# Delta-rule attention and GELU MLP on one NeuronCore: two units per join product, and the small products gathered into fewer stretches of TensorE work

## The chip, the cores and the metric

The kernel runs on one core of a Trainium2 chip. The metric is the device time of one execution in microseconds (us); the kernel before took 667.81 us, the median of 3 executions between 667.59 and 668.14. All the profile's times are of one profiled execution whose span was 667.6 us.

## The reference

Two blocks follow each other, all in float32. The first is a delta-rule recurrence for 4 batches x 8 heads, 768 steps, head size 48. The second is an MLP over the 3072 tokens, 384 -> 2048 -> 384, with an exact GELU.

```python
k_n = k / (norm(k) + 1e-06)
state = zeros(B, H, D, D)
for t in range(S):
    y[:, :, t] = q_t @ state
    v_old = state @ k_t
    state = state + beta_t * outer(k_t, v_t - v_old)
x = y.transpose(0, 2, 1, 3).reshape(B * S, H * D)
out = gelu(x @ w_in) @ w_out
```

## The kernel before, in words

**Chunks.** The 768 steps are cut into 12 chunks of C = 64. Within a chunk the recurrence is solved in closed form: the Gram matrix K K^T (`grams`), a unit triangular system built from it, the products of keys and queries with the running state (`against_state`), the solve itself (`solve`), the masked Q K^T (`queries`) times the solution, and the state's update (both in `outputs`, through `use`). A "unit" is one batch and head in one chunk. 32 units (2 chunks, 4 batches, 8 heads) make a group, and two batches lie above each other in the 128 partitions: partitions 0 to 63 hold one, 64 to 127 the other. In the code a tile index `u.a` is a pair of batches, `u.t` the place in the group, and `p` picks the half of the partitions.

**The triangular inverse.** For each group VectorE inverts all 32x32 diagonal blocks at once, one elimination row after another (`eliminate_steps`, L442 and L444). The missing off-diagonal 32x32 block of each unit is then made from two small products, the "joins". Level 0 multiplies the Gram block by the inverse of the upper diagonal block, and VectorE scales it into `xm` (L528). Level 1 multiplies that by the inverse of the lower block, and ScalarE copies it into the solve's matrix `zf` (L532). `join_steps` makes three calls of `join_run`: level 0 of the group's first chunk (call it J0), level 0 of its second chunk with level 1 of the first (J1), and level 1 of the second chunk (J2). Each product is a 32x32 by 32x32 matmul (L520).

**The MLP.** `fc1` (L684) makes 32 blocks of the hidden layer for a chunk's 256 tokens, each of three accumulating 128x128 by 128x256 matmuls. From chunk 2 on the second layer runs as seven block products (Strassen's scheme) of 16 matmuls of 128x128 by 128x192 each (L722). Its sums are on VectorE.

**Order.** `ffn_steps`, `state_steps`, `eliminate_steps` and the rest return lists of steps. `at(first, last, steps)` gives each a due time in chunks (w + 0.23 is about a quarter into the time of chunk w), and `emit` traces them all sorted by due time. VectorE then keeps exactly that order (`manual_schedule` for DVE). For TensorE and ScalarE the trace order is a priority: a list scheduler picks the first instruction that it holds ready. So a small product whose operand or PSUM buffer isn't free at that moment lets MLP matmuls in ahead of it, and a sequence of small products can come apart.

**PSUM.** All small products write into tiles tagged `dn` of two banks each, and there are two such tiles. A third one in flight waits until one has been read out. `queries`, `grams`, `solve` and each set of `join_run` take one; `against_state` and `use` take one per pair of batches, so two.

**In time of an even chunk w** the order is: J0 and the Gram product of chunk w+2 at w+0.23, J1 at w+0.30, J2 and Q K^T of chunk w at w+0.36, and then `state_steps`: keys and queries against the state (below: A), the solve (S), the outputs (O) and the transposition for the MLP. **In time of an odd chunk** it is the Gram product of chunk w+2 and Q K^T of chunk w at w+0.09, then A, S, O. Between these stand the MLP's matmuls. The keys reach the matmuls through a transposition on VectorE (`turned_k`, L352) into `Kt`, of which there are six buffers, two per chunk.

Of the kernel before, what the change touches and what calls it, by code (L numbers as in the profile page):

```python
# [11 lines left out]
ALU = mybir.AluOpType  # L12
# [4 lines left out]
def kernel(  # L17
# [28 lines left out]
    nc = tc.nc  # L46
    B, H, S, D = q.shape
    DM, DF = moe_w_in.shape
    C = 64
# [19 lines left out]
    def dn(name):  # L69
        return ps.tile([128, 2, 512], F32, tag="dn", name=name)  # L70
# [433 lines left out]
    def join_run(g, ts0, ts1):  # L504

        xm, zf, off = XMs[g], Zf[g % 2], Gs[g]
        gm = gms[g].rearrange("q t h -> q (t h)")
        sets = []
        for level, ts in enumerate((ts0, ts1)):
            if ts:  # L510
                psJ = dn("psJ")[:, 0].rearrange("q (u n) -> q u n", n=HB)
                sets.append((level, slice(ts[0] * H, (ts[-1] + 1) * H), psJ))
        for i in range(2 * H):
            for p in range(2):
                for level, us, psJ in sets:
                    u = us.start + i
                    top = slice(p * C, p * C + HB)
                    low_ = slice(p * C + HB, (p + 1) * C)
                    rows, to = (top, low_) if level == 0 else (low_, top)
                    nc.tensor.matmul(psJ[to, i, :], lhsT=(xm if level else off)[rows, u, :],  # L520
                                     rhs=zf[rows, u, HB:C] if level else xm[rows, u, :],
                                     start=True, stop=True)
        for level, us, psJ in sets:
            for p in range(2):
                top = slice(p * C, p * C + HB)
                low_ = slice(p * C + HB, (p + 1) * C)
                if level == 0:
                    nc.vector.tensor_tensor(  # L528
                        xm[low_, us, :], psJ[low_],
                        gm[low_, us].unsqueeze(2).to_broadcast([HB, 2 * H, HB]), op=ALU.mult)  # L530
                else:
                    nc.scalar.copy(zf[top, us, HB:C], psJ[top])  # L532
# [12 lines left out]

    def join_steps(g):
        a, b = range(NA), range(NA, 2 * NA)
        return [(1.0, join_run, g, a, ()), (1.0, join_run, g, b, a), (1.0, join_run, g, (), b)]
# [116 lines left out]
    def state_steps(c):  # L665
        us = [tiles[c, a] for a in range(NA)]
        steps = [(3.0, against_state, us), (2.0, solve, us), (3.0, outputs, us)]
        return steps + [(0.5, turn, u) for u in us]
# [258 lines left out]
    def late():  # L927
# [3 lines left out]
        for a in range(NA):  # L931
# [3 lines left out]
            for c in range(5, NC, 2):  # L935
# [11 lines left out]
             at(2.64, 2.77, join_steps(1)), at(2.76, 2.985, state_steps(2)),  # L947
# [6 lines left out]
    for c in range(4, NC):  # L954
# [8 lines left out]
        t = {4: 2.76, 5: 2.955}.get(c, c - (1.97 if c % 2 == 0 else 2.36))  # L963
        plan += [at(t, t + 0.01, [(1.0, turned_k, u) for u in us])]
        t = c + (0.05 if c % 2 == 0 else -0.34)
        plan += [at(t, t + 0.01, [(1.0, turned_q, u) for u in us])]
    for w in range(3, NC):
        us = [tiles[w, a] for a in range(NA)]
        two_ahead = w + 2 < NC
        gram = [(1.0, grams, [tiles[w + 2, a] for a in range(NA)])] if two_ahead else []  # L970
        query = [(1.0, queries, us)]
        if w == 3:
            gram = [(1.0, transposed, u, (1,)) for u in us] + gram
        if w % 2:
            plan += [at(w + 0.09, w + 0.092, gram + query), at(w + 0.25, w + 0.95, state_steps(w))]
# [6 lines left out]
        else:  # L982
            joins = join_steps(w // 2)
            plan += [at(w + 0.23, w + 0.232, joins[:1] + gram),
                     at(w + 0.3, w + 0.302, joins[1:2]),
                     at(w + 0.36, w + 0.362, joins[2:] + query),
                     at(w + 0.39, w + 0.97, state_steps(w))]
# [35 lines left out]
```

## Time and profile before

The chunks 4 to 9 form three alike periods of two chunks (an even chunk and the odd one after it), and 10 and 11 are a shorter fourth.

| stretch of the span, us | what | length | PE busy | DVE busy | ACT busy |
|---|---|---|---|---|---|
| 75 to 145 | MLP of chunks 0 and 1, chunk 1's state | 70.0 | 69.45 | 66.18 | 34.50 |
| 145 to 225 | joins of the first planned group, chunks 2 and 3 | 80.0 | 78.22 | 63.96 | 26.39 |
| 225 to 326, one period | chunks 4 and 5 | 101.0 | 100.88 | 69.34 | 31.09 |
| 528 to 625 | chunks 10 and 11, from the joins on | 97.0 | 96.88 | 39.78 | 24.63 |

PE is the matmul row of TensorE, DVE is VectorE, ACT is ScalarE. A matmul's recorded duration runs from its start to its modelled end, and matmuls overlap, so the space between two starts tells what one costs in a stream. The small matmuls on part of the array appear twice each in the records: a set of 32 join products is a group of x64. In a line of the timeline stand the start, the length from the first start to the last end, the engine, the line of the kernel, the operation, output and inputs, array rows * columns in use, the moving operand and the count.

### The profile page before, as it was taken

What the parts mean: (1) busy time and instruction counts of PE and PEld (TensorE: products, weight loads), DVE (VectorE), ACT (ScalarE), POOL (GpSimd) and SP (SyncE); (2) the same over time, 40 slices, a digit from 0 to 9 for tenths busy, and PEclk for the clock granted to TensorE, in tenths of its full rate; (3) what the DMA queues carried; (4) which work ended last, traced back from release to release, by engine and by line L of the source; (5) the groups of instructions that cost most, each with busy time, mean ns of one, the idle gap of its engine ahead of it and who ended that gap; (6) DMA issues with size and microseconds to landing.
All of it is one profiled execution on the core that took longest, in us unless ns stands there. A gap on an engine that the chain in (4) does not pass through costs nothing.

```text
span 667.6 us, 21705 instructions
## 1 busy us (share of the span) xinstructions
PE 643.4 (96%) x9542; PEld 563.6 (84%) x9542; DVE 451.9 (68%) x921; ACT 228.5 (34%) x605; POOL 82.3 (12%) x82
## 2 busy tenths in 40 slices
PE   6877999999999999999999999999999999999997
PEld 5666776767789989989989989989989989989997
DVE  6999999994799845489846489846479844324022
ACT  3367755704432242242143142143142132122220
POOL 4050300103110021111021111021111010000000
PEclk9966999998999999999999999999999999999999
DMA  9885655303432232511332511211301210100101
GB/s 132 175 253 173 121 170 133 48 1 71 83 45 39 51 52 43 85 32 26 57 53 45 82 27 31 51 19 32 67 3 26 56 18 3 25 2 2 24 1 25
DMA packets 158431, 39.76 MB, mean 60 GB/s; under 512 B 150016, under 2 KB 153216, under 8 KB 158336
## 3 DMA queue, kind: packets, MB, share of 16 engines
q1 hardware_dynamic: 152464, 33.40, 26.5%
q10 hardware_dynamic: 5872, 4.97, 3.3%
q8 instruction: 75, 1.23, 0.8%
q14 instruction: 20, 0.16, 0.1%
HBM read 33.62 MB, written 4.72 MB: 57 GB/s over the span
## 4 chain that ended last, share of the span: by engine, by line
PE 86%; DVE 7%; ACT 3%; issue 2%; DMA 1%; SPq 0%; DVEq 0%
PE psH L684 36%; PE psX L722 12%; PE psY L722 12%; PE psO L697 5%; PE psZ L722 4%; PE psK L575 3%; PE psJ L520 3%; PE psG L367 3%; PE psU L600 2%; PE psY L618 2%; DVE Nu L444 2%; DVE tmp L442 2%; PE psY L627 1%; ACT U L606 1%; PE psX L662 1%
## 5 line engine op out<-in xcount | busy, mean ns | idle before, releaser
L684 PE MATMUL psH<-xT,w_in_sb 128*128 128x256 f32 x1152 | 261.4, 383 | 2.4 <-ACT G L686 2.3
L684 PEld LDWEIGHTS psH<-xT,w_in_sb 128*128 128x128 f32 x1152 | 215.7, 190 | 33.7 <-ACT G L686 3.5
L686 ACT ACTIVATE G<-psH 128x256 f32<-128x256 f32 x192 | 73.3, 382 | 181.8 <-PE psH L684 169.8
L444 DVE TENSOR_TENSOR Nu<-Nu,tmp 128x30 f32<-128x30 f32 (+9 forms) x180 | 62.9, 349 | 6.2
L442 DVE TENSOR_TENSOR tmp<-Nu 128x30 f32<-128x30 f32 (+9 forms) x180 | 60.5, 336 | 5.1
L722 PE MATMUL psX<-w_out_sb,G 128*128 128x192 f32 x320 | 56.2, 329 | 0.0
L722 PE MATMUL psY<-w_out_sb,G 128*128 128x192 f32 x304 | 54.1, 329 | 0.6
L722 PEld LDWEIGHTS psX<-w_out_sb,G 128*128 128x128 f32 x320 | 52.2, 190 | 0.7
L722 PEld LDWEIGHTS psY<-w_out_sb,G 128*128 128x128 f32 x304 | 49.1, 190 | 2.1 <-DVE u L768 1.8
L663 ACT COPY xT<-psX 128x384 f32<-128x384 f32 x24 | 11.4, 478 | 105.0 <-PE psX L662 105.0
L697 PE MATMUL psO<-w_out_sb,G 128*128 128x384 f32 x128 | 45.0, 498 | 0.0
L306 POOL TENSOR_TENSOR n<-n,half 128x16 f32<-128x16 f32 x10 | 29.4, 2937 | 88.2 <-DVE n L281 67.4
L402 DVE TENSOR_TENSOR P<-psG,mask 128x1024 f32<-128x1024 f32 x10 | 12.2, 1224 | 37.0 <-PE psG L367 37.0
L606 ACT COPY U<-psU 64x192 f32<-64x192 f32 x96 | 30.0, 313 | 21.0 <-PE psU L600 19.7
L697 PEld LDWEIGHTS psO<-w_out_sb,G 128*128 128x128 f32 x128 | 23.7, 191 | 14.4 <-DVE w_out_sb L236 0.6
L583 DVE TENSOR_TENSOR W<-psK,V 128x384 f32<-128x384 f32 x22 | 12.1, 552 | 28.8 <-ACT y L582 28.8
L469 POOL MEMSET Zf<- 32x512 f32 x23 | 12.4, 540 | 154.5 <-DVE Zf L457 153.6
L731 DVE TENSOR_TENSOR S<-G 128x512 f32<-128x512 f32 x20 | 13.7, 687 | 25.8 <-ACT G L686 25.7
L332 POOL TENSOR_TENSOR V<-V,n 128x384 f32<-128x384 f32 x18 | 17.3, 968 | 104.5 <-DMA V<-in_v_dram 69.2
L641 DVE TENSOR_TENSOR x<-psY,y 64x192 f32<-64x192 f32 x80 | 28.3, 354 | 0.9
L722 PE MATMUL psY<-T,G 128*128 128x192 f32 x160 | 28.2, 329 | 0.0
L722 PE MATMUL psX<-T,G 128*128 128x192 f32 x160 | 28.1, 329 | 0.0
(138 smaller groups left out, 871.4 us busy)
## 6 DMA issues: line engine op xcount, KB each, us to landing
Kp<-in_k_dram SPq DMA_DIRECT2D x76, 96.0 KB, 3.3
w_out_sb<-in_moe_w_in_dram SPq DMA_DIRECT2D x24, 256.0 KB, 4.3
V<-in_v_dram SPq DMA_DIRECT2D x48, 96.0 KB, 3.1
out_dram<-o_sb ACTq DMA_DIRECT2D x46, 96.0 KB, 2.2
w_raw<-in_moe_w_out_dram SPq DMA_DIRECT2D x10, 384.0 KB, 4.7
Zf<-in_moe_w_out_dram SPq DMA_DIRECT2D x6, 384.0 KB, 3.9
Qp<-in_q_dram SPq DMA_DIRECT2D x64, 32.0 KB, 2.1
Qp<-in_q_dram SPq DMA_DIRECT2D x16, 96.0 KB, 4.2
```

Source lines behind the costliest of these rows:

```text
L306: nc.gpsimd.tensor_tensor(flat, flat, half, op=ALU.pow)
L367: nc.tensor.matmul(psG[HALF[p], r, i * NP + j, :], lhsT=u.Kt[rows, p, j, :], rhs=(u.Qt if x else u.Kt)[rows, p, j, :], start=True, stop=True)
L442: nc.vector.tensor_tensor(tmp, nu[:, j + 1:, j:j + 1].to_broadcast([128, n, j]), nu[:, j:j + 1, 0:j].to_broadcast([128, n, j]), op=ALU.mult)
L444: nc.vector.tensor_tensor(nu[:, j + 1:, 0:j], nu[:, j + 1:, 0:j], tmp, op=ALU.add)
L520: nc.tensor.matmul(psJ[to, i, :], lhsT=(xm if level else off)[rows, u, :], rhs=zf[rows, u, HB:C] if level else xm[rows, u, :], start=True, ...
L575: nc.tensor.matmul(u.psK[to, x, r, j, :], lhsT=(u.Qt if x else u.Kt)[rows, p, j, :], rhs=St[rows, u.a, p, j, :], start=True, stop=True)
L606: copy(pairs(u.U[HALF[p]], s), u.psU[HALF[p ^ s], p])
L641: nc.vector.tensor_tensor(dst, src, pairs(u.y[HALF[p ^ s]], s), op=ALU.add)
L684: nc.tensor.matmul(psH, lhsT=w_in_sb[:, f // 2, m, f % 2 * 128:(f % 2 + 1) * 128], rhs=xTs[c][:, m, :], start=(m == 0), stop=(m == NM - 1))
L686: nc.scalar.activation(G[:, f, :], psH, ACT.Gelu)
L697: nc.tensor.matmul(u.psO, lhsT=G[:, f, u.a * 128:(u.a + 1) * 128], rhs=w_out_sb[:, f, :], start=(f == 0), stop=(f == NF - 1))
L722: nc.tensor.matmul(ps_, lhsT=lhs[:, f, :], rhs=rhs[:, f, :], start=first and f == 0, stop=f == FH - 1, skip_group_check=not first)
```

## The change

One join product takes two units. The stationary operand is two neighbouring units' blocks side by side (32 rows, 64 columns) and the moving operand two units' blocks (64 columns). Of the 64x64 result only the two 32x32 blocks on the diagonal are wanted. This halves the number of join matmuls. Both levels of J1 share one `dn` tile, a bank each, and the readouts take every other unit, twice as many instructions with half the elements each.

The helper `together` records for each TensorE instruction of its steps a dependence on the one before it, for order alone and with no semaphore, so that they are issued in this sequence. With it the small products are placed anew. Even chunk: J0 with Q K^T of w, J1 with the Gram product of w+2, J2 with A, S with the Gram product of w+3, O. Odd chunk: A, S with Q K^T of w, O. The keys of odd chunks are transposed a little earlier (c - 2.49 in place of c - 2.36). For chunk 3 the two transpositions of its queries stand ahead of the Gram product of chunk 5, and for the first planned group each join call is kept together by itself.

```diff
@@ join_run
-                psJ = dn("psJ")[:, 0].rearrange("q (u n) -> q u n", n=HB)
-                sets.append((level, slice(ts[0] * H, (ts[-1] + 1) * H), psJ))
-        for i in range(2 * H):
+        psJ = dn("psJ").rearrange("q b (k n) -> q b k n", n=2 * HB)
+        sets = [(level, ts[0] * H, psJ[:, level])
+                for level, ts in enumerate((ts0, ts1)) if ts]
+        for k in range(H):
             for p in range(2):
-                for level, us, psJ in sets:
-                    u = us.start + i
+                for level, u0, psJ in reversed(sets):
+                    us = slice(u0 + 2 * k, u0 + 2 * k + 2)
+                    rows = slice(p * C + level * HB, p * C + (level + 1) * HB)
+                    nc.tensor.matmul(psJ[HALF[p], k, :],
+                                     lhsT=(xm if level else off)[rows, us, :],
+                                     rhs=zf[rows, us, HB:C] if level else xm[rows, us, :],
...
+                for e in range(2):
+                    us = slice(u0 + e, u0 + 2 * H, 2)
+                    src = psJ[at_:at_ + HB, :, e * HB:(e + 1) * HB]
...
@@ together (new)
+        run = [next(i for i in reversed(traced) if i.engine == pe)]
...
+        for before, i in zip(run, run[1:]):
+            tc.add_manual_dep(i, before.name,
+                              mybir.DependencyInfo(mybir.DependencyClass.NoSync,
+                                                   mybir.DependencyReason.DATA),
...
@@ state_steps
-        steps = [(3.0, against_state, us), (2.0, solve, us), (3.0, outputs, us)]
+        steps = [(3.0, together, *first, (against_state, us)),
+                 (2.0, together, (solve, us), *second), (3.0, outputs, us)]
@@ the plan, odd chunks
-            plan += [at(w + 0.09, w + 0.092, gram + query), at(w + 0.25, w + 0.95, state_steps(w))]
+            plan += [at(w + 0.25, w + 0.95, state_steps(w, (), query(w)))]
@@ the plan, even chunks
-            plan += [at(w + 0.23, w + 0.232, joins[:1] + gram),
-                     at(w + 0.3, w + 0.302, joins[1:2]),
-                     at(w + 0.36, w + 0.362, joins[2:] + query),
-                     at(w + 0.39, w + 0.97, state_steps(w))]
+            plan += [at(w + 0.23, w + 0.232, [(1.0, together, j0, *query(w))]),
+                     at(w + 0.35, w + 0.351, [(1.0, together, j1, *gram(w + 2))]),
+                     at(w + 0.39, w + 0.97, state_steps(w, (j2,), gram(w + 3)))]
```

## The prediction, made before the changed kernel was run

> **What bounds the kernel now.** I read the page's busy shares first, then the table by stretches, TensorE's waits from 80 us on, and the timeline of TensorE. The page:
>
> ```profile
> PE 643.4 (96%) x9542; PEld 563.6 (84%) x9542; DVE 451.9 (68%) x921; ACT 228.5 (34%) x605; POOL 82.3 (12%) x82
> ```
>
> The stretches of the three alike periods (length, then PE, PEld, DVE, ACT, POOL busy):
>
> ```profile
> 225.00:326.00 101.00, 100.88 (x1582) 91.70 (x1581) 69.34 (x149) 31.09 (x76) 14.03 (x11) 1.00 0.30 49
> 326.00:427.00 101.00, 100.88 (x1582) 91.70 (x1581) 69.35 (x149) 31.10 (x76) 13.73 (x11) 1.00 0.30 49
> 427.00:528.00 101.00, 100.88 (x1582) 91.70 (x1581) 69.30 (x149) 30.14 (x74) 13.52 (x11) 1.00 0.19 33
> ```
>
> What TensorE waited for after 80 us:
>
> ```profile
> PE psJ L520 <- issue: 1.2, 1, 1.2
> PE psH L684 <- ACT G L686: 0.3, 1, 0.3
> ```
>
> The reader sees a period of 101.0 us with TensorE busy for all of it, at full clock, and under 2 us of matmul waits in the whole rest. Every us of TensorE's stream that goes away shortens the kernel, as long as no other engine takes over; VectorE has 32 us to spare in a period. But a busy row also holds drains and changes between array shapes. Those the timeline shows, by starts:
>
> ```profile
> 437.54 1.16 PE L367 MATMUL psG<-Kt 48*64 48x64 f32 x64
> 438.63 2.86 PE L684 MATMUL psH<-xT,w_in_sb 128*128 128x256 f32 x12
> 441.42 1.20 PE L520 MATMUL psJ<-XM,G 32*32 32x32 f32 x64
> 442.55 1.56 PE L684 MATMUL psH<-xT,w_in_sb 128*128 128x256 f32 x6
> 444.04 1.20 PE L520 MATMUL psJ<-Zf,XM 32*32 32x32 f32 x64
> ...
> 448.89 5.45 PE L684 MATMUL psH<-xT,w_in_sb 128*128 128x256 f32 x24
> 454.26 0.68 PE L575 MATMUL psK<-St,Kt 48*64 48x48 f32 x32
> 454.77 0.65 PE L575 MATMUL psK<-St,Qt 48*64 48x48 f32 x32
> 455.23 0.65 PE L575 MATMUL psK<-St,Kt 48*64 48x48 f32 x32
> 455.70 0.65 PE L575 MATMUL psK<-St,Qt 48*64 48x48 f32 x32
> ...
> 462.97 1.15 PE L600 MATMUL psU<-W,Zf 64*64 64x48 f32 x64
> 464.05 2.87 PE L722 MATMUL psX<-w_out_sb,G 128*128 128x192 f32 x16
> ```
>
> Three prices come from it. (1) *The MLP side of an interruption.* 24 first-layer matmuls take 454.26 - 448.89 = 5.37 us, 12 take 441.42 - 438.63 = 2.79, so one is 0.215 us and a stretch between two small runs has 2.79 - 12 x 0.215 = 0.20 us on top. (2) *The small side.* A block of 32 records of A takes 455.23 - 454.77 = 0.46 us, so 64 are 0.93; S, with 64, takes 464.05 - 462.97 = 1.08. Entry and exit are 0.15 us. An interruption thus costs 0.35 us beside its products. (3) *A join set.* 64 records take 442.55 - 441.42 = 1.13 us, about 1.01 of stream and 0.12 of exit.
>
> The joins have a telling exception near the end, where the two levels of J1 alternate:
>
> ```profile
> 541.33 0.21 PE L520 MATMUL psJ<-XM,G 32*32 32x32 f32 x1
> 541.34 0.21 PE L520 MATMUL psJ<-Zf,XM 32*32 32x32 f32 x1
> ...
> 542.43 0.19 PE L520 MATMUL psJ<-Zf,XM 32*32 32x32 f32 x1
> 542.55 2.86 PE L684 MATMUL psH<-xT,w_in_sb 128*128 128x256 f32 x12
> ```
>
> Here 128 records take 1.10 us to the last start, 8.6 ns each, where a lone level takes 16.0. A lone level uses two parts of the array (rows 0 and 64 upward), J1 uses four. So a part repeats every 32 to 34 ns either way: a lone join set is bound by its two parts, not by the number of instructions.
>
> **What the Trainium skill says.** "TensorE: Matmul & The Clock Gate", section "The mechanism", has weight loads overlap running matmuls only on other row groups; the 2 against 4 parts above agree. Its section "LDWEIGHTS (loading the stationary operand)" prices a load by its columns alone, columns / 1.2 ns: an estimate of 27 ns for 32 columns and 53 for 64. The trace has 32 ns per part at 32 columns; at 64 columns (A, S, O, the Gram product, four parts) 0.46 us / 32 x 4 = 58 ns with a block's seam. Both are the page's figure plus about 5, so I trust the slope. "TensorEngine Tiling (Array Packing)", "Key Properties", says that a change of tiling mode drains the array; the 0.35 us agree in kind.
>
> **The change, part by part.**
>
> *Half the join matmuls.* J0 falls from 64 records to 32 on the same two parts, but each loads 64 columns and streams 64. Not shown by the trace: 64 columns with 32 rows, where no second column part shares the rows. Bounds for a part's repeat: 32 ns if nothing grows with width, 75 if load and stream are added in full to today's 32 (32 + 27 + 16). I take 55, the value of the 64x64 products without a seam, between the page's 53 and the measured 58. Then J0 is 32 / 2 x 55 = 0.88 us, J1 64 / 4 x 55 = 0.88, J2 0.88; with exit 1.0 each. Halving the count therefore gives a lone set only 0.13 us. What gives more is that J1 stays whole: in three periods it is split today (the lines at 441.42 and 444.04), because it takes two `dn` tiles while the Gram product of w+2 holds one until J1 has let go of the old Gram matrix. Afterwards it takes one tile and the Gram product follows it. Four sets at 1.13 = 4.52 become three at 1.0: 1.5 us per period.
>
> *Fewer interruptions.* Today a period has 12: J0 with Gram, J1b, J1a, J2 with Q K^T, A, S, O; then a scrap of eight Gram records, Gram with Q K^T, A, S, O. The change asks for 8, with one more change of shape inside (J2 to A), about 0.14 us. But J2 with A wants three `dn` tiles: J2's and two of A. J2's must be read by four ScalarE copies first; today's two of 32x512 take 1.15 us, so four of half the size about 1.45. A's second half would be due 0.95 us after J2's end, so it comes some 0.6 us early. Either MLP matmuls slip in (a ninth interruption, 0.35) or TensorE waits 0.6. I take the former. Saving: 3 x 0.35 - 0.14 = 0.9 us. A period gains 1.5 + 0.9 = 2.4, less 0.1 for the seams inside S with Gram and S with Q K^T: 2.3. Three periods: 6.9.
>
> *Chunks 2 and 3.* The joins there have 256 records in 4.4 us (2.15 + 1.13 + 1.13); three sets at 1.0 save 1.4. The Gram product of chunk 5 now stands in three scraps between transpositions and Q K^T alone behind it; whole, and Q K^T behind S, saves about 3 x 0.35 = 1.0.
>
> *Chunks 10 and 11.* J1 is whole already: 1.13 + 1.22 + 1.13 become 3.0, 0.5 saved; 11 interruptions become 8 or 9, less the shape change: 0.5.
>
> Sum: 6.9 + 1.4 + 1.0 + 0.5 + 0.5 = 10.3 us, so 667.8 - 10.3 = 657.5.
>
> *Costed at nothing.* The readouts double in number. VectorE's two of 690 ns become four of about 0.42 (a 128x240 product takes 0.41): 0.3 us more, twice a period, in its 32 spare us, and J1 follows J0 by over 4 us of MLP work. ScalarE, a third busy, has 0.3 more per level 1. The earlier Gram product of w+3 needs `Kt` from VectorE at w+0.51, whose buffer A of w frees; VectorE has just waited for that A for its own W (L583), so it adds no wait. Behind S, Q K^T is read by VectorE (1.22 us) in its fixed order; elimination rows queue behind that, and the joins behind them, but today XM is ready at 433.0 and J0 starts at 436.4: 3.4 us of room. No wait is recorded by `together`, only order.
>
> **The rivals.** (a) *The narrow tile is faster than I take it* (a part repeats in 32 to 45 ns, because load and stream overlap): at 32 ns each set is 0.51, so 15 x 0.37 = 5.6 us more, 652; at 45, 655. For it: no other operation here uses these tiles. Against it: columns set the price of everything in the trace. (b) *The joins gain nothing* (75 ns, 1.2 per set, so 15 x 0.32 = 4.8 less), or as much is lost in waits of A's second half: 662. (c) *Waits take the place*: a chained run stands whole while ScalarE is behind. If J2's readout queues behind the Gram copies (442.67 to 445.01, 2.3 us) and its own 1.45, each of the four even chunks loses about 3.8 us at A. A is then not split, so the gain is 10.3 + 4 x 0.35 = 11.7 and the time 667.8 - 11.7 + 15.2 = 671, slower than before. Against it: some 5 us of MLP work lie between J1 and J2, in which ScalarE can finish the Gram copies.
>
> **How the numbers follow.** My case (with A split or briefly waiting, 656 to 659) 0.58; (a) 0.20; (b) 0.12; (c) together with smaller losses that eat most of the gain 0.10, over half of it beyond 669. The range leaves out the fastest end of (a) and the waits of (c): 652 to 663. Chances: faster 0.90, same 0.04, slower 0.06.
>
> **What would show it.** The changed timeline should have join sets of 32, 64 and 32 records at 0.9 to 1.0 us; 8 or 9 interruptions in a period of 98.7 us; J1 directly before the Gram product; MLP matmuls or 0.6 us of idle time inside A of the even chunks. A join set at 0.5 us speaks for (a). Waits of psK, psJ or psY on ScalarE, or of the joins on VectorE's rows, above 3 us a period would make the prediction wrong.

## The result, and the profile after

The changed kernel takes 670.80 us (median of 4 executions, 670.35 to 671.38); the kernel before took 667.97 us beside it (4 executions, 667.59 to 669.34). The ratio is 1.0037, with a 95% interval of 1.0023 to 1.0052. The change makes the kernel slower by 0.4%, where the prediction had 657.5 us and a range that ended at 663.

The page of the changed kernel, engines:

```profile
PE 634.2 (95%) x8902; PEld 554.6 (83%) x8902; DVE 454.1 (68%) x941; ACT 231.2 (35%) x625; POOL 82.1 (12%) x82
```

TensorE has 640 records fewer (9542 before) and is busy 9.2 us less (643.4 before), yet the span grew from 667.6 to 668.6 us. So work did go away, and waits took its place.

The counts in these views are records. Every matmul on float32 data stands there as two records, the large ones too, and a transposition as one: the code has 16 blocks of the hidden layer in a chunk, not 32, with three matmuls each, so 576 in all, and the view has 1152 records; a second-layer product has 8 matmuls and 16 records. Below, numbers of first-layer matmuls are numbers of records: six make one block, and each block is emptied by one GELU out of one of two PSUM tiles.

A stretch of one of the alike periods (length, then PE, PEld, DVE, ACT, POOL busy) shows where:

```profile
225.00:326.00 101.00, 99.21 (x1452) 90.10 (x1452) 69.02 (x153) 31.61 (x80) 13.79 (x11) 1.00 0.30 48
```

In the same 101.0 us TensorE is now busy for 99.21 and not for 100.88. What it waited for after 80 us, in the changed kernel (total, times, longest, us):

```profile
PE psH L700 <- ACT G L702: 3.1, 4, 0.9
PE psK L590 <- ACT Zf L532: 2.0, 4, 0.5
PE psJ L516 <- DVE XM L528: 1.6, 1, 1.6
```

Each of the first two lines comes four times, once for every even chunk from 4 on. L700 is the MLP's first layer, held up by the GELU (L702) that empties its PSUM tile. L590 is A, the products against the state, held up by the readout of J2 (L532). The third is J1 in the time of chunk 2.

The timeline of TensorE in the changed kernel, the even chunk whose former order the prediction showed:

```profile
437.13 1.15 PE L516 MATMUL psJ<-XM,G 32*64 32x64 f32 x32
438.21 1.16 PE L367 MATMUL psG<-Qt,Kt 48*64 48x64 f32 x64
439.30 5.45 PE L700 MATMUL psH<-xT,w_in_sb 128*128 128x256 f32 x24
444.68 0.27 PE L516 MATMUL psJ<-Zf,XM 32*64 32x64 f32 x1
...
445.76 1.16 PE L367 MATMUL psG<-Kt 48*64 48x64 f32 x64
446.86 2.86 PE L700 MATMUL psH<-xT,w_in_sb 128*128 128x256 f32 x12
450.63 3.24 PE L700 MATMUL psH<-xT,w_in_sb 128*128 128x256 f32 x12 [0.92 <-ACT G L702]
453.80 1.15 PE L516 MATMUL psJ<-Zf,XM 32*64 32x64 f32 x32
454.88 0.68 PE L590 MATMUL psK<-St,Kt 48*64 48x48 f32 x32
455.38 0.65 PE L590 MATMUL psK<-St,Qt 48*64 48x48 f32 x32
456.53 0.68 PE L590 MATMUL psK<-St,Kt 48*64 48x48 f32 x32 [0.51 <-ACT Zf L532]
```

The order is the one that was asked for: J0 with Q K^T, J1 with the Gram product, J2 with A. J0 takes 438.21 - 437.13 = 1.08 us, J1 (both levels, 64 records) 445.76 - 444.68 = 1.08, J2 1.08; each of them had been 1.13 per level. Two things are new. The 24 first-layer matmuls after the Gram product take 453.80 - 446.86 = 6.94 us, where 24 undisturbed ones, at 439.30 to 444.68, take 5.38: 1.56 us of waiting. And A's second half starts at 456.53, 1.15 us after the block before it, where blocks follow each other in 0.46 to 0.50.

One wait more shows later in the period, in the second layer of the changed kernel:

```profile
479.04 0.49 PE L677 MATMUL psX<-ident,x 128*128 128x128 f32 x3
479.65 0.92 PE L738 MATMUL psY<-w_out_sb,G 128*128 128x192 f32 x4
```

and of the kernel before, the same place:

```profile
476.76 0.49 PE L662 MATMUL psX<-ident,x 128*128 128x128 f32 x3
477.18 0.34 PE L367 MATMUL psG<-Kt 48*64 48x64 f32 x8
477.46 0.59 PE L722 MATMUL psY<-w_out_sb,G 128*128 128x192 f32 x2
```

Before, a scrap of eight Gram records stood behind the three transpositions. Now nothing does, and the next second-layer product starts late. Its operands have long been there; VectorE's read (L784) of the block of PSUM that this product overwrites ends at 479.60, just before it. That scrap, which the prediction counted as an interruption to be saved, stood where a wait shows now.

**The account of one period**, from the starts in both timelines. From J0 to J0 it was 101.01 us and is 101.33.

| term, us per period | before | after | difference |
|---|---|---|---|
| runs of small products, without A's wait | 19.09 | 17.56 | -1.53 |
| MLP side of the interruptions, 0.197 each | 12 | 8 | -0.79 |
| first layer waits behind J1 and Gram | 0 | 1.56 | +1.56 |
| A's second half waits for J2's readout | 0 | 0.69 | +0.69 |
| second layer waits where the scrap was | 0 | 0.39 | +0.39 |
| sum | | | +0.32 |

The first, third and fourth rows are read from the starts. The price of 0.197 us is the one of the kernel before, and the 0.39 us are what then remains of the large matmuls' time between O of the even chunk and A of the odd one, so these two rows are not measured apart. With that, the gain is there, 2.32 us, and 2.64 us of waits stand against it. Three periods make +0.96 of the 1.0 us by which the span grew. Chunks 2 and 3 add 0.08 (88.75 us from the first planned J0 to the next, now 88.83), and chunks 10 and 11 nothing (123.97 and 123.96 us from their J0 to the last product).

The medians differ by 2.83 us and not by 1.0, since the profiled execution of the kernel before was, by its span, the longest of its four (669.34 us), and that of the changed kernel (670.35) the shortest. Part of it shows in the record of the kernel before, with a granted clock of 0.95 from 145 to 180 us (1.00 in the changed kernel): Q K^T at 153.90 takes 1.90 us from start to start there, and 1.09 elsewhere. So the 0.08 us of chunks 2 and 3 are likely too small a loss. The lengths of the periods, which all lie at full clock, are free of this and are what the experiments are read by.

### The profile page after: what moved, and what is told of

It is laid out like the page before. It is cut to its first block, busy times and chain, and to the rows that moved or that the text cites. A ratio compares the mean times of both kernels' runs of the same rounds, so it can differ in the third digit from the quotient of the medians.

```text
span 668.6 us, 20459 instructions
## 1 busy us (share of the span) xinstructions
PE 634.2 (95%) x8902; PEld 554.6 (83%) x8902; DVE 454.1 (68%) x941; ACT 231.2 (35%) x625; POOL 82.1 (12%) x82
## 3 DMA queue, kind: packets, MB, share of 16 engines
q8 instruction: 70, 1.15, 0.7%
## 4 chain that ended last, share of the span: by engine, by line
PE 73%; DVE 15%; ACT 5%; issue 3%; DMA 2%; SPq 1%; POOL 0%; ACTq 0%; POOLq 0%; DVEq 0%
PE psH L700 31%; PE psX L738 12%; PE psY L738 12%; PE psZ L738 4%; DVE tmp L442 3%; DVE Nu L444 3%; PE psK L590 3%; PE psJ L516 2%; PE psG L367 2%; PE psU L615 2%; ACT Zf L532 2%; PE psY L633 1%; DVE w_e L235 1%; DVE w_out_sb L236 1%; PE psY L642 1%
## 5 line engine op out<-in xcount | busy, mean ns | idle before, releaser
L700 PE MATMUL psH<-xT,w_in_sb 128*128 128x256 f32 x1152 | 261.2, 383 | 5.4 <-ACT G L702 4.5
L700 PEld LDWEIGHTS psH<-xT,w_in_sb 128*128 128x128 f32 x1152 | 216.4, 191 | 39.4 <-ACT G L702 8.8
L702 ACT ACTIVATE G<-psH 128x256 f32<-128x256 f32 x192 | 73.5, 383 | 175.9 <-PE psH L700 156.4
L528 DVE TENSOR_TENSOR XM<-psJ,gm 32x256 f32<-32x256 f32 x40 | 16.8, 421 | 25.1 <-PE psJ L516 24.7
L752 DVE TENSOR_TENSOR G<-G 128x512 f32<-128x512 f32 x20 | 13.8, 692 | 24.2 <-PE psX L738 24.2
```

What stands on the lines that cost most here:

```text
L528: nc.vector.tensor_tensor(xm[low_, us, :], src, gm[low_, us].unsqueeze(2).to_broadcast([HB, H, HB]), op=ALU.mult)
L700: nc.tensor.matmul(psH, lhsT=w_in_sb[:, f // 2, m, f % 2 * 128:(f % 2 + 1) * 128], rhs=xTs[c][:, m, :], start=(m == 0), stop=(m == NM - 1))
L702: nc.scalar.activation(G[:, f, :], psH, ACT.Gelu)
```

## The experiments

Theory 1 was: the readouts of J1 on ScalarE hold up the GELUs behind them. The rivals were: the narrow tile itself is too slow to gain anything (2); the chained runs cost what the waits of A show (3). Later, theory 1 was taken apart into what ScalarE waits for and what stands ahead of the GELUs in its queue.

### The joins alone, in the old order

The kernel before, with nothing but the changed `join_run`:

```diff
-        for i in range(2 * H):
+        for k in range(H):
...
-                    nc.tensor.matmul(psJ[to, i, :], lhsT=(xm if level else off)[rows, u, :],
+                    nc.tensor.matmul(psJ[HALF[p], k, :],
+                                     lhsT=(xm if level else off)[rows, us, :],
```

> The kernel before, with only the joins changed: two units per product, both levels of J1 in one dn tile; order and grouping as before. Theory (ScalarE's queue ate the gain, the narrow tile is sound): three join sets of 1.08 us in place of four of 1.13 and one interruption fewer, 1.5 us per period saved, less up to 1 us where the first layer waits behind J1's and the Gram product's copies: 662 to 666 us against 668 for the kernel before. Rival (the 32x64 tile itself costs too much): no faster than the kernel before.

It takes 665.31 us (664.80 to 665.69), a ratio of 0.9958 (0.9943 to 0.9973): faster. The length and engines of a period:

```profile
234.54:334.24 99.70, 99.48 (x1453) 90.48 (x1452) 70.21 (x154) 31.65 (x80) 13.78 (x11) 1.00 0.30 50
```

99.70 us is 1.31 less than before, in each of the three periods. The runs of small products fall from 19.10 to 17.96 us, and the MLP has one interruption less, about 0.2. The small side is J1 in one piece (1.09 in place of twice 1.13), 0.05 less for J0, and 0.11 more for J2 with Q K^T, which now starts 1.24 us behind it. The tile costs 1.08 us for 32 records on two parts, so rival 2 falls. The view of waits lists none of TensorE between 225 and 528 us, although J1 shares its PSUM tile and has the doubled readouts here too. The timeline of ScalarE in this kernel tells why:

```profile
241.83 1.24 ACT L385 COPY diag<-G 32x512 f32<-32x512 f32 x2
243.09 1.48 ACT L532 COPY Zf<-psJ 32x256 f32<-32x256 f32 x4
244.59 0.66 ACT L686 ACTIVATE G<-psH 128x256 f32<-128x256 f32 x2
```

In the old order the Gram product stands with J0, so its copies come first. By the time ScalarE reaches J1's readout, VectorE is through with its share (at 242.47), and ScalarE doesn't wait. It still has nearly 4 us of copies ahead of its GELUs (240.72 to 244.57), and they cost nothing. Behind J1 stand only 12 first-layer matmuls (240.59 to 243.38), two blocks, as many as the first layer has PSUM tiles. Then 2.33 us of J2 and Q K^T follow, and both GELUs are done before the first layer goes on at 245.71. In the changed kernel 24 first-layer matmuls in one piece follow J1 and the Gram product. The loss must come from the new placing.

### One unit per product, in the new order

The changed kernel with 32x32 products, both levels of J1 in one tile as in the change, and two readouts of 32x512 per level:

```diff
-        for k in range(H):
+        for i in range(2 * H):
...
-                                     lhsT=(xm if level else off)[rows, us, :],
+                    nc.tensor.matmul(psJ[to, i, :], lhsT=(xm if level else off)[rows, u, :],
...
-                        nc.scalar.copy(zf[p * C:p * C + HB, us, HB:C], src)
+                    nc.scalar.copy(zf[top, us, HB:C], psJ[top])
```

> The changed kernel with one unit per join product again (32x32), both levels of J1 still in one dn tile, readouts two of 32x512 again. Theory: lone join sets take 1.13 in place of 1.08 us, but the level 1 readouts are 0.34 us shorter, so the waits of the first layer and of A fall by about 0.3 each: some 0.5 us per period, 1.5 to 2 us below the changed kernel. Rival (the narrow tile): the loss of the change is gone, 6 us or more below the changed kernel.

It takes 677.49 us (673.56 to 680.02), 1.0136 (1.0092 to 1.0179): a miss, far slower than the changed kernel. Timeline of TensorE:

```profile
244.23 2.86 PE L699 MATMUL psH<-xT,w_in_sb 128*128 128x256 f32 x12
249.25 4.43 PE L699 MATMUL psH<-xT,w_in_sb 128*128 128x256 f32 x12 [2.17 <-ACT G L701]
253.62 1.25 PE L518 MATMUL psJ<-Zf,XM 32*32 32x32 f32 x64
```

The same 24 matmuls of the first layer take 253.62 - 244.23 = 9.39 us, 4.0 more than undisturbed. ScalarE at the same place, one period later:

```profile
350.75 1.16 ACT L531 COPY Zf<-psJ 32x512 f32<-32x512 f32 x2 [2.32 <-DVE XM L527]
...
352.88 0.54 ACT L278 ACTIVATE ksq<-Kp 128x384 f32<-128x384 f32 x1
353.44 1.24 ACT L385 COPY diag<-G 32x512 f32<-32x512 f32 x2
354.71 0.66 ACT L701 ACTIVATE G<-psH 128x256 f32<-128x256 f32 x2
```

ScalarE stands still for 2.32 us ahead of the readout, and then does 354.71 - 350.75 = 3.96 us of copies and a square before the two GELUs, behind which the first layer waits with both of its PSUM tiles full. So the new order costs time with either tile, and the expectation failed because it took this wait to be tied to the doubled readouts. It is not. Nor does the difference to the changed kernel speak for the wider tile: here the scheduler has put all four Gram copies and a square ahead of the GELUs, there only two Gram copies stand ahead of the first one.

### Who reads J1

The timeline of ScalarE in the changed kernel, at the place shown above:

```profile
447.72 1.49 ACT L532 COPY Zf<-psJ 32x256 f32<-32x256 f32 x4 [2.55 <-DVE XM L528]
449.22 0.59 ACT L378 COPY G<-psG 128x512 f32<-128x512 f32 x1
449.70 0.59 ACT L382 COPY diag<-psG 128x512 f32<-128x512 f32 x1
450.18 0.40 ACT L702 ACTIVATE G<-psH 128x256 f32<-128x256 f32 x1
450.60 1.24 ACT L385 COPY diag<-G 32x512 f32<-32x512 f32 x2
```

and VectorE's:

```profile
445.90 1.73 DVE L528 TENSOR_TENSOR XM<-psJ,gm 32x256 f32<-32x256 f32 x4 [4.60 <-PE psJ L516]
```

The Gram matmuls begin at 445.76, when J1 is over on TensorE. VectorE reads level 0 from 445.90 to 447.63, and only then does ScalarE read level 1, from 447.72. The two levels lie in different banks of one tile, and the data of level 1 don't depend on VectorE's reading. But in the compiled program ScalarE's copy waits for it: the code lists level 0 first, and the second reader of a tile follows the first. Of the 2.55 us that ScalarE stands idle, about 1.8 lie behind the end of J1. The instructions behind the readout stand still too: two Gram copies ahead of the first GELU, two more (L385) ahead of the second. The kernel before shows the other case, near its end, where both levels of J1 run together but in two `dn` tiles:

```profile
542.65 1.41 DVE L528 TENSOR_TENSOR XM<-psJ,gm 32x512 f32<-32x512 f32 x2 [2.59 <-PE psJ L520]
542.69 1.16 ACT L532 COPY Zf<-psJ 32x512 f32<-32x512 f32 x2 [0.87 <-PE psJ L520]
```

There the two engines read side by side.

Three experiments change the reader or the order of the readers. In the first VectorE does both of J1's readouts:

```diff
-                        nc.scalar.copy(zf[p * C:p * C + HB, us, HB:C], src)
+                        (nc.vector.tensor_copy if len(sets) == 2 else nc.scalar.copy)(
+                            zf[p * C:p * C + HB, us, HB:C], src)
```

> The changed kernel, but J1's level 1 block is copied by VectorE in place of ScalarE (J2's still by ScalarE). Theory (the first layer waits because ScalarE has 1.49 us of J1's copies and 2.4 us of Gram copies ahead of its GELUs): the 1.56 us that the 24 first-layer matmuls after J1 lose falls below 0.4; A's wait of 0.69 us stays; 3 to 5 us below the changed kernel. Rival (VectorE or order bounds there): the gap stays or moves to the joins.

It takes 666.44 us (9 executions, 665.75 to 667.72), 0.9977 (0.9967 to 0.9986); the period falls from 101.33 to 100.12. TensorE:

```profile
243.19 5.80 PE L701 MATMUL psH<-xT,w_in_sb 128*128 128x256 f32 x24
248.92 1.15 PE L516 MATMUL psJ<-Zf,XM 32*64 32x64 f32 x32
```

The 24 matmuls take 5.73 us: of 1.56 us of waiting 0.35 are left. The first layer's wait does come from J1's readout on ScalarE.

In the second ScalarE keeps the readout and does it first:

```diff
-        for level, u0, psJ in sets:
+        for level, u0, psJ in reversed(sets):
             for p in range(2):
                 for e in range(2):
```

> The changed kernel with one thing swapped: of J1's two blocks, which share a dn tile, ScalarE's (level 1) is read out first and VectorE's (level 0) after it. Theory (the two readouts of a tile are made to follow each other, so ScalarE stands 2 us with its copies behind VectorE's 1.73, and the Gram copies and GELUs stand behind those): ScalarE begins right after J1, the 1.56 us that the first layer loses per period fall below 0.3, VectorE's readout moves 1.5 us later and nobody waits for it; 3.5 to 5.5 us below the changed kernel. Rival (ScalarE simply has too much work there, 3.9 us of copies): the wait stays above 1 us and the time within 1.5 us of the changed kernel.

It takes 667.09 us (12 executions, 666.39 to 669.55), 0.9990 (0.9979 to 1.0000), 3.7 less than the changed kernel; the period is 100.54. ScalarE and TensorE:

```profile
343.58 1.49 ACT L532 COPY Zf<-psJ 32x256 f32<-32x256 f32 x4 [0.74 <-PE psJ L516]
...
346.19 1.24 ACT L385 COPY diag<-G 32x512 f32<-32x512 f32 x2
347.46 0.38 ACT L702 ACTIVATE G<-psH 128x256 f32<-128x256 f32 x1
```

```profile
344.53 2.86 PE L700 MATMUL psH<-xT,w_in_sb 128*128 128x256 f32 x12
347.90 2.86 PE L700 MATMUL psH<-xT,w_in_sb 128*128 128x256 f32 x12 [0.51 <-ACT G L702]
350.69 1.15 PE L516 MATMUL psJ<-Zf,XM 32*64 32x64 f32 x32
```

ScalarE no longer waits for VectorE (VectorE now follows it, from 345.10), and the 24 matmuls take 350.69 - 344.53 = 6.16 us. So the wait falls by 0.78 of the 1.56 us; below 0.3 was expected, so this is half a miss. The other 0.78 remain: between the readout and the GELU there are 2.4 us of Gram copies. The split is that of these two runs: the scheduler has also put L385 ahead of the first GELU here, where it stood behind it in the changed kernel.

In the third the 32x32 products of the second experiment get the same reversed readout, to see whether it is the tile or the order of the readers:

```diff
-        for level, u0, psJ in sets:
+        for level, u0, psJ in reversed(sets):
             us = slice(u0, u0 + 2 * H)
```

> The new plan with one unit per product (which took 677.5 us), now with J1's level 1 read out first. It asks why that run was slow. In its program the scheduler put all the Gram copies and one square ahead of the GELUs that the first layer waits for, and they all stood behind VectorE's readout. Theory (ScalarE's queue behind VectorE is the cause, not the form of the matmuls): some 1.4 us come off the wait of 4.0 us in each of three periods, 671 to 674 us; since the order of the queue is as unlucky as before, it stays above the changed kernel. Rival (32x32 products themselves disturb the new plan): no change from 677.

674.28 us (672.98 to 674.61), 1.0095 (1.0082 to 1.0108), and the first layer's wait falls from 4.0 to 1.9 us in the first period. The same edit helps there too; the time lies just above the 671 to 674 us that were expected.

### J2's readout, and J2's place

A waits 0.69 us in every even chunk for J2's readout. Half of it given to VectorE:

```diff
-                        nc.scalar.copy(zf[p * C:p * C + HB, us, HB:C], src)
+                        (nc.vector.tensor_copy if len(sets) == 1 and p else nc.scalar.copy)(
+                            zf[p * C:p * C + HB, us, HB:C], src)
```

> The changed kernel, but the upper half of the partitions of J2's block is copied by VectorE and only the lower by ScalarE. Theory (A's second half waits for J2's dn tile until ScalarE has made four copies): A's wait of 0.69 us falls below 0.1 in the four even chunks, 2 to 3 us below the changed kernel; the first layer's wait stays. Rival (A waits for something else): no change.

671.14 us (670.00 to 673.18), 1.0045 (1.0026 to 1.0065): a miss, nothing gained. Timeline of all engines:

```profile
355.07 0.74 ACT L532 COPY Zf<-psJ 32x256 f32<-32x256 f32 x2 [0.70 <-PE psJ L516]
355.84 0.86 DVE L532 COPY Zf<-psJ 32x256 f32<-32x256 f32 x2 [3.74 <-ACT Zf L532]
356.85 0.68 PE L591 MATMUL psK<-St,Kt 48*64 48x48 f32 x32 [0.75 <-DVE Zf L532]
```

The two halves don't run beside each other: VectorE begins at 355.84, when ScalarE has ended at 355.81. Here too the second reader of a tile follows the first, and the idle time listed for A grows from 0.51 to 0.75. It is the same order of readers as at J1.

J2 taken out of A's run and put in on its own:

```diff
-                     at(w + 0.39, w + 0.97, state_steps(w, (j2,), gram(w + 3)))]
+                     at(w + 0.36, w + 0.362, [(1.0, together, j2)]),
+                     at(w + 0.39, w + 0.97, state_steps(w, (), gram(w + 3)))]
```

> The changed kernel with J2 taken out of A's run and put alone at w+0.36. Theory: A's wait of 0.69 us goes, one interruption of about 0.35 comes back, in four even chunks: 1 to 2 us below the changed kernel, if J2's copies do not lengthen the first layer's wait. Rival (A's wait hides other waiting): no change.

675.41 us (674.29 to 678.40), 1.0118 (1.0091 to 1.0145): a miss. TensorE:

```profile
247.37 1.15 PE L516 MATMUL psJ<-Zf,XM 32*64 32x64 f32 x32 [1.27 <-ACT Zf L532]
...
252.19 2.86 PE L700 MATMUL psH<-xT,w_in_sb 128*128 128x256 f32 x12 [1.75 <-ACT G L702]
```

A's wait is gone, but w + 0.36 lies only four first-layer matmuls behind J1 at w + 0.351, so J2 itself waits for J1's readout (1.27 us), and the first layer waits longer than before (1.75). With the reversed readout as well:

```diff
-        for level, u0, psJ in sets:
+        for level, u0, psJ in reversed(sets):
...
-                     at(w + 0.39, w + 0.97, state_steps(w, (j2,), gram(w + 3)))]
+                     at(w + 0.36, w + 0.362, [(1.0, together, j2)]),
+                     at(w + 0.39, w + 0.97, state_steps(w, (), gram(w + 3)))]
```

> Both of these: level 1 read first, J2 apart from A. Theory: the gains add up, 5 to 7 us below the changed kernel, 664 to 666 us, so below the kernel before too. Rival (another queue takes over): no better than the better of the two.

672.15 us (670.26 to 672.85), 1.0058 (1.0038 to 1.0078): a miss too. Now VectorE is the later reader, and J2 waits for its product instead, 1.3 us a period. These two runs did not separate A's wait from the rest, since the place that was chosen for J2 was bad; they show that four first-layer matmuls are too little distance between J1 and J2.

### What stands ahead of the GELUs

The remaining 0.78 us of the first layer's wait, with level 1 read first. The last Gram copies (L385, 1.24 us) go to GpSimd, on top of the reversed readout:

```diff
-                nc.scalar.copy(Ds[g][lower, span], Gs[g][lower, span])
+                nc.gpsimd.tensor_copy(Ds[g][lower, span], Gs[g][lower, span])
```

> The changed kernel with level 1 read first (667.1 us), and the Gram's last two copies (SBUF to SBUF, 1.24 us per Gram product) moved from ScalarE to GpSimd. It asks what the first layer still waits for there, 0.77 us per period. Theory (the mere amount of copies ahead of the GELU on ScalarE: 1.49 + 1.17 + 1.24): with 1.24 gone the wait falls below 0.2, a period takes 99.8 to 100.0 us in place of 100.5, 664.5 to 666 us. Rival (the Gram copies are not what the GELU waits for): 667.

674.36 us (673.34 to 674.55), 1.0096 (1.0083 to 1.0109): a miss. The stretch from the first planned J0 to the next is 93.10 us in place of 88.59, so most of the loss is outside the periods (VectorE's elimination, L434, waits 3.4 us there for GpSimd's copies); a period is 100.93, also more than 100.54. ScalarE:

```profile
353.40 0.52 ACT L278 ACTIVATE ksq<-Kp 128x384 f32<-128x384 f32 x1 [1.28 <-DVE n L281]
353.83 0.36 ACT L702 ACTIVATE G<-psH 128x256 f32<-128x256 f32 x1
```

The copies are gone, and a square of the next keys has come up in their place. It waits 1.28 us for VectorE (its buffer's last reduction), and the GELU stands behind it: 1.16 us of first-layer wait. So both have to leave. Also on top of the reversed readout, GpSimd now makes the copies for the first chunk of each group from group 3 on (groups counted from 0, so in the time of chunk 4 and later), and the squares and their sums come later:

```diff
-                nc.scalar.copy(Ds[g][lower, span], Gs[g][lower, span])
+                (nc.gpsimd.tensor_copy if us[0].t == 0 and g > 2 else nc.scalar.copy)(Ds[g][lower, span], Gs[g][lower, span])
...
-                plan += [at(w + 0.35, w + 0.36, [(1.0, prep, w + 2)]),
-                         at(w + 0.5, w + 0.51, [(1.0, finish, w + 2)])]
+                plan += [at(w + 0.42, w + 0.43, [(1.0, prep, w + 2)]),
+                         at(w + 0.56, w + 0.57, [(1.0, finish, w + 2)])]
```

In this kernel and the next the squares of an even chunk come after the following chunk's keys have been loaded into the same buffer, so these two kernels leave out the even chunks' own norms and take those of the following chunk's keys; the instructions and their shapes are the same.

> Level 1 read first, the last Gram copies on GpSimd for the later even chunks (groups after the second), and the squares of the next keys later (w+0.42 in place of w+0.35, their factors at w+0.56), so that no instruction that waits for VectorE stands ahead of the GELUs. Theory (0.77 us are made of 1.24 us of copies and of the squares' place in the queue): the wait of the first layer behind J1 falls below 0.2 us, periods of 99.8 to 100.0 us, 664.5 to 666 us. Rival (something else delays the GELU): 100.5 us as before.

665.06 us (664.66 to 665.36), 0.9957 (0.9945 to 0.9970). TensorE:

```profile
342.62 5.45 PE L700 MATMUL psH<-xT,w_in_sb 128*128 128x256 f32 x24
347.99 1.15 PE L516 MATMUL psJ<-Zf,XM 32*64 32x64 f32 x32
```

The 24 matmuls take 5.37 us, undisturbed. The period is 99.95 in the mean (99.94, 100.16 and 99.76). The later squares alone, with the copies back on ScalarE:

```diff
-                (nc.gpsimd.tensor_copy if us[0].t == 0 and g > 2 else nc.scalar.copy)(Ds[g][lower, span], Gs[g][lower, span])
+                nc.scalar.copy(Ds[g][lower, span], Gs[g][lower, span])
```

> Level 1 read first and the squares later, the Gram copies all on ScalarE. Theory: 3.9 us of copies still stand ahead of the GELUs, so the wait stays at 0.7 to 0.9 us and a period at 100.4 to 100.6. Rival (the squares alone are the cause): below 0.3 us.

667.54 us (12 executions, 666.74 to 669.26), 0.9998 (0.9990 to 1.0007). The 24 matmuls take 6.15 us, as with the squares in their old place. So the Gram copies alone are enough to keep the wait of 0.78, the squares alone are enough to keep one as well, and it goes when neither stands ahead of the GELU.

These runs also test the account. Gross gain and the two other waits give a period of 101.01 - 2.32 + 0.69 + 0.39 = 99.77 with no first-layer wait (99.95 was measured with both gone), and with 0.78 of it 100.55 (measured with level 1 first: 100.54).

### Parts of the new order

The old order for even chunks, the new for odd ones, with the new products:

```diff
-            plan += [at(w + 0.23, w + 0.232, [(1.0, together, j0, *query(w))]),
-                     at(w + 0.35, w + 0.351, [(1.0, together, j1, *gram(w + 2))]),
-                     at(w + 0.39, w + 0.97, state_steps(w, (j2,), gram(w + 3)))]
+            one = lambda steps: [(1.0, *s) for s in steps]
+            plan += [at(w + 0.23, w + 0.232, one([j0] + gram(w + 2))),
+                     at(w + 0.3, w + 0.302, one([j1])),
+                     at(w + 0.36, w + 0.362, one([j2] + query(w))),
+                     at(w + 0.39, w + 0.97, state_steps(w, (), gram(w + 3)))]
```

> Joins of two units in the old order of the even chunks (J0 with Gram w+2, J1, J2 with Q K^T, A) and the new order of the rest (S with Gram w+3; S with Q K^T). It tells what the regrouping of the odd chunks is worth by itself, against the run of the joins alone (665.3 us). Theory (fewer interruptions save 0.2 us each on the MLP's side and 0.15 on their own, but the scrap of Gram products filled a wait of the second layer for VectorE, which now shows as 0.39): 0.2 to 0.5 us per period, 664 to 665. Rival (interruptions are worth their full 0.35, three of them): 661 to 662.

664.81 us (663.61 to 666.18), 0.9953 (0.9936 to 0.9969). That is 0.5 below the joins alone, within the scatter of both. Its three periods are 100.75, 99.65 and 99.40, against 99.70 for each of the joins alone; the first one holds a wait of 0.7 us for the copy of the MLP's input. The even chunks' new order is what costs: without it 6.0 us of the changed kernel's time are gone. What the odd chunks' order is worth by itself stays unsettled in this run.

In that kernel J1 of the first planned group still waits 1.63 us for VectorE's product, in the time of chunk 2. Two runs move these joins apart:

```diff
-             at(2.64, 2.77, [(1.0, together, j) for j in join_steps(1)]), at(2.76, 2.985, state_steps(2)),
+             at(2.5, 2.77, [(1.0, together, j) for j in join_steps(1)]), at(2.76, 2.985, state_steps(2)),
```

> A try for a version faster than both: two-unit joins, old order of the even chunks, new order of the rest, and the first planned group's three joins spread over the time of chunk 2 from 2.5 (before 2.64) to 2.77, so that J1 and J2 no longer wait for the readout of the join before them (1.65 and 0.8 us of idle time there in the version without the spread). Theory (those waits are on the path): 1.5 to 2.5 us below that version's 664.8, so 662.3 to 663.3. Rival (the time is lost again at the next wait of chunk 2): 664.5 or more.

667.57 us (14 executions, 666.03 to 669.09), 1.0000 (0.9991 to 1.0009): a miss. J0 came before VectorE's elimination was through and held TensorE for 4.2 us (L453, `back`, writes its operand). To the other side:

```diff
-             at(2.64, 2.77, [(1.0, together, j) for j in join_steps(1)]), at(2.76, 2.985, state_steps(2)),
+             at(2.64, 2.85, [(1.0, together, j) for j in join_steps(1)]), at(2.76, 2.985, state_steps(2)),
```

> Two-unit joins, old order of the even chunks, new order of the rest, and the first planned group's joins spread to a later end (2.64 to 2.85 in place of 2.77). Theory (J1 and J2 wait there for the readout of the join before them, 1.65 and 0.8 us): 1 to 2.5 us below the version without the spread (664.8). Rival (the solve of chunk 2 then waits for J2's copies, so the time is given back): 664.5 to 665.5.

661.80 us (6 executions, 660.79 to 663.14) against 667.58 beside it: 0.9911 (0.9895 to 0.9927). This version beats both kernels, and it is 3.0 us below the one that it is made from, where 1 to 2.5 were expected. TensorE in the time of chunk 2:

```profile
145.54 1.15 PE L516 MATMUL psJ<-XM,G 32*64 32x64 f32 x32
146.62 2.85 PE L713 MATMUL psO<-w_out_sb,G 128*128 128x384 f32 x8
149.40 1.16 PE L367 MATMUL psG<-Qt,Kt 48*64 48x64 f32 x64
```

Eight records of the MLP's output matmuls and Q K^T now lie between J0 and J1 (at 150.72), and J2 came behind A (at 157.39). The waits of J1 and J2 (1.63 and 0.7 us) are gone, and the stretch from the first planned J0 to the next takes 86.22 us where that of the kernel it is made from took 88.86. Another 1.2 us come from the first period, which is 99.53 here and had been 100.75; the others are as before (99.63 and 99.40).

## Why the prediction was wrong

**What bounds the kernel.** TensorE's stream does bound it, and the joins alone show it: 1.14 us less of small products and one interruption less, about 0.2, shortened a period by 1.31. The condition that the prediction put, "as long as no other engine takes over", is the one that failed. No engine took over as a whole. One queue did, ScalarE's, for 1.56 + 0.69 = 2.25 us behind J1 and J2 in each period. (The waits in the view of before, most of them not shown, add up to 2.1 us, not to under 2.)

**The join sets.** The direction and the mechanism were right: a part of the array repeats in 60 ns with 64 columns (1.08 less 0.12 of exit, over 16), and J1 in one piece is where the gain is. The size was a little off: a set takes 1.08 and not 1.0, as the repeat is 58 to 60 ns and not 55. The higher of the two neighbouring values, the 58 ns with a block's seam, would have been the better choice. The joins gave 1.3 us per period instead of 1.5. Rival (a), the fast narrow tile, has no support; rival (b), 1.2 per set, was nearer than (a) for the tile itself. The 16 ns of streaming in its bound of 75 are not worked out there; by the timeline of before a record of 256 columns costs 0.215 us and one of 192 columns 2.60 / 16 = 0.163, which is 26 ns for 32 columns.

**The Trainium skill.** The slope by columns of "LDWEIGHTS (loading the stationary operand)" held: an estimate of 53 ns for 64 columns by the page's formula and 58 to 60 measured, as 27 and 32 for 32 columns. The reading of A as four parts needs more than the prediction said, though: its four parts lie on two halves of the rows and two of the columns, and a half of the rows takes a record every 0.46 us / 32 x 2 = 29 ns, less than the estimate for one load. So the loads of A overlapped between column halves as well, and not on other rows only.

**The interruptions.** There are 8, as asked for. The price of 0.197 us on the MLP side was taken over, not measured anew. With it the gross gain of joins and interruptions together is 2.32 us per period. The prediction, taking its sum without the split of A, had 2.3 + 0.35 = 2.65. This part was right within 13%.

**The step that failed is "Costed at nothing".** It said of ScalarE, "a third busy", that it "has 0.3 more per level 1". That is a statement about the share of busy time, and the share is still a third (31.61 us in 101). What counted was the order: which instruction stands ahead of the GELU that frees a PSUM tile of the first layer, what that instruction itself waits for, and how many first-layer matmuls come before the next small products. With J1 and the Gram product in one run, four readouts of J1 and two Gram copies stood ahead of the first GELU and two more copies ahead of the second, and the first of the readouts waited for VectorE through the shared tile, about 1.8 us beyond the end of J1. The prediction named the merging of J1 into one `dn` tile only as a gain, and the same tile makes the two readers follow each other. Cost: 1.56 us per period. Half of it went when ScalarE no longer waited for VectorE, the other half when the last Gram copies and the squares had left as well. In the old order the same copies cost nothing, behind 12 first-layer matmuls in place of 24.

**A's wait.** 0.6 us was worked out, and 0.69 came. It was foreseen as the alternative, but the split was taken: with `together` no MLP matmul may come in between.

**The scrap.** Eight Gram records counted as an interruption saved, with nothing said of what they filled; 0.39 us of the second layer's wait came to light. This is the remainder of the account, and no run put the scrap back alone. The last experiment supports it: against the joins alone its periods differ by the new order of S and the odd chunks, with two interruptions less. The small side fell by 0.26 us, as it should; the MLP side, where 0.39 should have gone, rose by 0.08.

**Chunks 2 and 3.** 2.4 us were expected to be gained and 0.08 were lost, although the profile of before was slowed there, so that the real loss is probably larger. J1 waits 1.6 us and J2 0.7 us for readouts, and eat the gain; before, the only wait of the joins there was 1.2 us; the last experiment, which spaces them, took 2.64 us out of this stretch. The prediction looked for room between J0 and J1 only in the later periods ("J1 follows J0 by over 4 us of MLP work"), and in the first group only four records of output matmuls stand there. Before, level 0 of both chunks ran there in one go (128 records at 145.65), so only level 1 had to wait for VectorE; with both levels of J1 in one run the whole of J1 waits.

**The rivals.** Rival (c), at 671 us and slower than before, is what happened, with the time almost met. That match is luck: it set 15.2 us of loss against 11.7 of gain, and the three periods had 7.9 against 7.0. Its place was only partly right: it had J2's readout behind the Gram copies, with a loss of 3.8 us at A. What came was the first layer's GELU behind J1's readout and the same copies; A lost 0.69. The argument against it, that "some 5 us of MLP work lie between J1 and J2, in which ScalarE can finish the Gram copies", overlooked that this MLP work needs ScalarE itself, for a GELU every six records, with two PSUM tiles between them.

## What to carry to other kernels

Work taken out of the bounding engine's stream is won only where the in-order queue of the engine that frees its buffers keeps up at that very place: read the timeline of that engine, see what will stand ahead of the freeing instruction and what that waits for, and don't read its share of busy time. In this compiled program two engines that read one PSUM tile follow each other in the order of the code, even from different banks, so the one with the more urgent queue behind it should be listed first, or the data lie in two tiles. Scraps and interruptions that look like waste may fill a wait or give a slower queue the time to catch up, and short sets of dependent products want some work between them.

## What the runs showed of the hardware beyond what was expected

A record on 32 rows with 64 columns repeats every 60 ns on one part of the array (0.96 us over 16), where one with 32 columns takes 32. So halving the number of join products saves only 0.05 us per lone set (1.13 to 1.08): the width sets the price, not the count. Weights and moving operand were widened together; S, whose moving operand has 48 columns, and Q K^T, with 64, take 1.08 and 1.09 us with weights of 64 columns, which speaks for the weights.

A readout that is cut in two, with every other unit in each, isn't free: on ScalarE two copies of 32x512 take 1.15 us and four of 32x256 take 1.49; on VectorE two products took 690 ns each and four of half the size take 0.42 each (1.73 us together).
